# Moving the bit work of one weight pair, the scaling of low words, and the low half of an attention result in a fused attention and two-MLP kernel

## The chip, the cores and the metric

The kernel runs on one core of a Trainium2 chip. The metric is the device time of one execution in microseconds (us). Five engines work on their own instruction queues, each in order: TensorE (PE, with its weight loads shown as PEld), VectorE (DVE), ScalarE (ACT), GpSimd (POOL) and SyncE (SP), which issues the DMAs. An instruction starts when those before it on its queue are done and the semaphores that it waits for have come.

## The reference

All data are fp32; a local attention is followed by two feed-forward stages:

```
for each chunk c of 32 tokens (B=4, H=8, S=768, D=64):
    keys, values = 8 memory rows + 16 tokens to the left, the chunk, 8 to the right
    a = exp(scores - max(scores));  a = a / (sum(a) + 1e-9)
    out[c] = a @ values
x = out as 3072 tokens x 512
h = max(x @ w1, x @ w2, x @ w3)            # 512 -> 768
x = h @ w_mid                              # 768 -> 512
g = x @ w_in                               # 512 -> 2048
g = g where g >= 1, 0 where g <= -1, else (g + 1)^2 / 4
result = g @ w_out                         # 2048 -> 512
```

The weights (`w1`, `w2`, `w3`, `w_mid`, `w_in`, `w_out`) come in as float64 and are read by the kernel as pairs of 32-bit words, a low and a high one, from which it makes fp32.

## The kernel before

The 3072 tokens are six blocks of 512 (`TB`), and each block is four attention units of 128 tokens. The main matmuls are split in two halves: `mm3` (L538 to L541) multiplies high by high, low by high and high by low, so each product takes three matmuls of 128x512.

Blocks and units run like this. Attention units 0 to 7 and layer 1 of block 0 follow a written list (`PLAN`). Then a loop (L1088) goes over *slots*. A slot is one of the three layer-1 products of a sixth of the hidden width (`slot_l1`, with m = 0, 1, 2: twelve matmuls into one of two PSUM banks taken in turn by `next_mm`), or one layer-2 step (`slot_l2`, twelve matmuls). For m = 0 ACT copies the bank to `t` (L572), for m = 1 and 2 DVE takes the maximum with `t` (L574); the second slot of layer 1 after this one needs the bank again. After m = 2, in the next slot, ACT rounds `t` to `hh_a` (L556) and POOL subtracts to get `hl_a` (L558).

Behind its matmuls each slot of blocks 1 to 4 gets one step of an attention unit (`att_step`, `steps`; slots 2 and 3 get two), and the steps of one unit are six: (0) output `o` of the unit before on PE (L457), scores `s` on PE (L393), high half `cx` on ACT (L475), then on DVE the maximum and its subtraction `mx` (L407, L408) and the low half `dx` (L479), and on ACT the exponential `ex` (L412); (1) the normalising `n` on DVE (L416 to L419); (2) the rearrangement `pc` on ACT (L424, L427) and transposes for the next unit; (3) the transpose `ta` of the probabilities on DVE (L431), which `o` of the next step 0 reads; (4) and (5) little. The four `o` and `s` results share PSUM banks 4 and 5. Units 8 to 23 run here; the units whose step 0 lies in this loop are 9 to 23.

Beside it, `round_step` turns one pair of weight tiles in six slots into fp32, 16 pairs (12 to 27) in all. Action "a" takes absolute values of the high words on ACT (`abs_w`, L135), scales the low words on ACT (`tail_w`, L139) and works on the bits on DVE (`bits_w`, L143 to L146). Action "b" adds the low words on DVE (`sum_w`, L151) and combines (L159 to L162, or L176 to L179). `BY_PART` says which action falls to which of the six parts; "in" fetches the next weights, "out" stores the last, "p" splits a finished one on ACT (L169) and POOL (L170). The attention step comes ahead of `round_step` in a slot. Outside the pattern, "a" of pair 12 is put into slot 1 and its "b" into slot 3. In slots 0 and 1 ACT also empties four PSUM banks of block 0 (L605).

After block 4 the loop handles the last block without attention, and then the second feed-forward runs on PE to the end.

Of the kernel before, what the change touches and what calls it, by code (L numbers as in the profile page):

```python
# [65 lines left out]
def attention_then_two_mlps(ctx, tc, q, k, v, mem_k, mem_v, w1, w2, w3, w_mid, w_in, w_out, out):  # L66
# [17 lines left out]
    mx = ctx.enter_context(tc.tile_pool(name="mx", bufs=2))  # L84
# [25 lines left out]
    staged, split2, tiles = {}, {}, {}  # L110

    def fetch_w(n):
        q, i = divmod(n, 2)
        kind, j = conv[n]
        src = wsrc[kind]
        if q not in staged:
            staged[q] = stage.tile([P, 2, TB, 2], U32, tag="st", name=f"st{q}", bufs=2)
        st = staged[q][:, i]
        if kind in ("b", "d"):
            nc.sync.dma_start(out=st.rearrange("p f t -> p (f t)"), in_=src[j * P:(j + 1) * P, :])  # L120
        else:
            nc.sync.dma_start(
                out=st.rearrange("p (k f) t -> p k (f t)", k=KD),
                in_=src[:, 2 * j * P:2 * (j + 1) * P].rearrange("(k p) f -> p k f", p=P),
            )
# [8 lines left out]
    def abs_w(q, c):  # L134
        nc.scalar.activation(out=c.bitcast(F32), in_=staged[q][:, :, :, 1].bitcast(F32), func=AF.Abs)  # L135

    def tail_w(q):
        low = staged[q][:, :, :, 0]
        nc.scalar.activation(out=low, in_=low, func=AF.Copy, scale=2.0 ** -29)  # L139

    def bits_w(q, c):
        V, cf = nc.vector, c.bitcast(F32)
        V.tensor_scalar(out=cf, in0=cf, scalar1=LEAST, scalar2=MOST, op0=ALU.max, op1=ALU.min)  # L143
        V.tensor_scalar(out=c, in0=c, scalar1=3, scalar2=0x3FFFFFFF,
                        op0=ALU.logical_shift_left, op1=ALU.bitwise_and)
        V.scalar_tensor_tensor(out=c, in0=staged[q][:, :, :, 1], scalar=0xC0000000, in1=c,  # L146
                               op0=ALU.bitwise_and, op1=ALU.bitwise_or)

    def sum_w(q, c):
        st = staged.pop(q)  # L150
        nc.vector.tensor_tensor(out=c, in0=c, in1=st[:, :, :, 0], op=ALU.add)  # L151
        return st
# [12 lines left out]
    def streamed_d(c, d):  # L165

        for i, x in (0, d[:, 0:2]), (2, c[:, :, HK:]):
            hi = d[:, 3 + i:5 + i]
            nc.scalar.copy(out=hi.bitcast(F32R), in_=x)  # L169
            nc.gpsimd.tensor_tensor(out=x.bitcast(F32R), in0=x, in1=hi, op=ALU.subtract)  # L170
# [11 lines left out]
    def new_c(q):  # L182
        tiles[q] = stage.tile([P, 2, TB], U32, tag="c", name=f"c{q}", bufs=2)
        return tiles[q]
# [305 lines left out]
    def steps(u):  # L490
        old = u + 1 < TRIO0
        late = not old and u % 3 == 2
        if u == UB:
            yield [("s", u), ("mx", u), ("ex", u)]
        else:
            yield [("o", u - 1), ("s", u), ("cx", u - 1), ("mx", u), ("dx", u - 1), ("ex", u)]
        m = [("n", u)] + [("mv", u)] * (u % UPB == 0 or u == TURN0) + [("lv", u)]
        if old:
            v = [("tk", u + 2), ("ck", u + 2), ("ek", u + 2)] if u + 2 < TRIO0 else []
            v += [("lk", u + 4)] if u + 4 < TRIO0 else []  # L500
            yield m + v + [("kw", u + 1)]
            v = [("tq", u + 1), ("cq", u + 1)]
            v += [("lq", u + 3)] if u + 3 < TRIO0 else []
        else:
            yield m
            v = [("fk", u + 1)] * (not late)
        if u + 2 >= TRIO0:
            v += [("fq", u + 2)]
        if u == TRIO0 - 3 or u >= TRIO0 - 2 and u % 2 == 0:
            v += [("gq", u // 2 + 2)]  # L510
        if u >= TRIO0 - 2 and u % 3 == 1:
            v += [("gk", u // 3 + 1)]
        yield ([("pc", u)] if u >= TURN0 else []) + v
        yield [("ta", u)] if u >= TURN0 else [("a", u), ("ca", u)]
        new = u % UPB == 0
        yield [("fk", u + 1)] * late
        yield [("lm", u // UPB + 1)] if new and u < TURN0 else []
        if u == NU - 1:
            yield [("o", u), ("cx", u), ("dx", u)]
# [466 lines left out]
    def round_step(acts):  # L986
        if "out" in acts and kept:
            q, c, d = kept.pop(0)
            if q < Q2:
                f = q - Q1  # L990
                nc.sync.dma_start(out=sd[f], in_=d[:, 0:7])
                nc.sync.dma_start(out=sc[f].rearrange("p m f -> p (m f)"), in_=c.rearrange("p i f -> p (i f)"))
            else:
                nc.sync.dma_start(out=cd[q - Q2][:, 0:4].rearrange("p m f -> p (m f)"), in_=c.rearrange("p i f -> p (i f)"))
                nc.sync.dma_start(out=cd[q - Q2][:, 4:7], in_=d)
        if "p" in acts and kept and kept[0][0] < Q2:
            streamed_d(*kept[0][1:])
        q = rounded[0]
        if "a" in acts and q in staged:
            abs_w(q, new_c(q))  # L1000
            tail_w(q)
            bits_w(q, tiles[q])
        if "b" in acts and q in tiles:
            st = sum_w(q, tiles[q])
            c = tiles.pop(q).bitcast(F32)
            kept.append((q, c, (combine_d if q < Q2 else combine_w)(st, c)))
            rounded[0] += 1
        if "in" in acts:
            for _ in range(acts.count("in")):
                if fetched[0] < len(conv) and fetched[0] // 2 - rounded[0] < 2:  # L1010
                    fetch_w(fetched[0])
                    fetched[0] += 1

    BY_PART = "", "p", "", "out a", "in in", "b"

    with tc.manual_schedule(engines={ENG.PE, ENG.DVE, ENG.Activation, ENG.Pool, ENG.SP}):
        memk = at.tile([P, B // 2, 2, D], F32, tag="p", name="memk", bufs=2)
# [70 lines left out]
        for s, (f, *a) in enumerate(order):  # L1088
            j = a[0]
            if f is not slot_l2 and j == NB - 1 and last_block == 0:  # L1090
                while todo:
                    att_step()
                att.close()
                rp = ctx.enter_context(tc.tile_pool(name="rp", bufs=1, side="right"))
                last_block = s
                hb.append(rp.tile([P, TB], F32R, tag="hb0", name="hb0"))
                hb.extend(mx.tile([P, TB], F32R, tag="y", name=f"hb{i}", bufs=2) for i in (1, 2))
                fb.extend(rp.tile([P, TB], F32, tag=f"f{i}", name=f"f{i}") for i in range(6))
                hq["h12", 2] = [rp.tile([P, TB], F32, tag=f"h{i}", name=f"h12_{i}") for i in (4, 5)]
                for g in (0, 1):  # L1100
                    hq["h22", g] = rp.tile([P, 2, TB], F32, tag=f"a{g}", name=f"h22_{g}")
            made, out_now = unsplit[:], stores[:]
            del stores[:]
            f(*a)
            if last_block:
                made = unsplit[:]
            else:

                for _ in range(2 if s in (2, 3) else 1):
                    att_step()  # L1110
                    done += 1
                for _ in range(2):
                    if evictions:
                        evictions.pop(0)()

            for x in made:
                l1_split(*x)
                unsplit.remove(x)
            if last_block:
                t = s - last_block  # L1120
                round_step(["out"])
                if t == 1:
                    for g in (2, 3):
                        hq["h22", g] = w_tile(f"h22_{g}")
                for name in LAST_BLOCK.get(t, "").split():
                    if name == "c":
                        split_c()
                    elif name == "raw":
                        load_c(loaded[0])
                        loaded[0] += 1  # L1130
                    elif name == "r":
                        load_d(t - 4)
                    elif name == "d":
                        i = len(resident)
                        split_d(i)
                        if i + 2 < len(RESIDENT):
                            load_d(i + 2)
                    elif name == "E":
                        hq["h21", 0] = w_tile("h21_0")
                    else:  # L1140
                        prep(0, name)
            else:
                part = 5 if s == 3 else done % 6
                feed((5, 6, 4, 6, 5, 1)[part])
                round_step(BY_PART[part].split() + (["a"] if s == 1 else []))
                for store in out_now:
                    store()
        for x in unsplit:
# [81 lines left out]
```

## Time and profile before

| | |
|---|---|
| median of 3 runs | 962.69 us (959.14, 962.69 and 962.74) |
| profiled execution, its own time | 958.58 us |
| span of that execution, first to last instruction | 956.8 us |
| PE busy | 933.4 us, 98% of the span |
| DVE, ACT, POOL busy | 715.3, 569.9, 339.1 us |
| mean granted TensorE clock | 0.994 of full speed |

Times in the rows below are from the start of the span. PE's idle time is 23.4 us of the span. In a timeline row the first number is the start, the second the duration; in square brackets stands the idle time ahead of the instruction and what ended it. Slots 0 to 94 of the loop lie from about 125 to 423 us.

### The profile page before, as it was taken

How to read it: one execution, taken by the hardware profiler on the slowest of the kernel's cores; microseconds unless marked ns; L12 is line 12 of the kernel's file. 1: busy time of each engine (PE TensorE's matmuls, PEld its weight loads, DVE VectorE, ACT ScalarE, POOL GpSimd, SP SyncE). 2: the span in 40 equal slices, each digit the busy share in tenths (PEclk: the TensorE clock that was granted, in tenths of full speed). 3: DMA queues.
4: the chain of work that ended last, by engine and by line, in shares of the span. 5: the costliest groups of instructions: out<-in, count | busy, mean ns of one | idle time of the engine just before them, and what ended most of it. 6: DMA issues, size and time to landing. Idle time of an engine off the chain costs nothing.

```text
span 956.8 us, 18726 instructions
## 1 busy us (share of the span) xinstructions
PE 933.4 (98%) x7026; PEld 767.3 (80%) x7026; DVE 715.3 (75%) x1017; ACT 569.9 (60%) x1036; POOL 339.1 (35%) x330
## 2 busy tenths in 40 slices
PE   6799989999999999999999999999999999999998
PEld 5588877878888888888888888888888888888886
DVE  3999848788887878753337778997777998777854
ACT  5767544554454345333347777776777776776763
POOL 0000002322321111111646665555665555655542
PEclk8999999999999999999999999999999999999999
DMA  7896625776858677333424239514326744232823
GB/s 179 237 223 208 193 83 159 178 211 193 215 143 207 173 191 240 111 132 110 138 65 128 78 93 304 159 34 111 99 78 211 213 113 102 83 94 86 261 67 66
DMA packets 245548, 142.82 MB, mean 149 GB/s; under 512 B 174290, under 2 KB 223186, under 8 KB 245458
## 3 DMA queue, kind: packets, MB, share of 16 engines
q1 hardware_dynamic: 245458, 141.63, 52.7%
q8 instruction: 55, 0.90, 0.4%
q14 instruction: 35, 0.29, 0.1%
HBM read 109.87 MB, written 31.46 MB: 148 GB/s over the span
## 4 chain that ended last, share of the span: by engine, by line
PE 91%; DVE 4%; ACT 2%; SPq 1%; issue 1%; DMA 1%; POOL 0%; DVEq 0%; POOLq 0%; ACTq 0%
PE psums L539 29%; PE psums L541 28%; PE psums L540 28%; PE psums L393 2%; PE psums L457 2%; DMA kq<-in_k_dram 1%; PE psums L288 1%; DVE c L151 0%; PE psums L1051 0%; PE psums L464 0%; SPq L983 0%; SPq L375 0%; DVE p L408 0%; DVE few L407 0%; ACT c L135 0%
## 5 line engine op out<-in xcount | busy, mean ns | idle before, releaser
L558 POOL TENSOR_TENSOR hl_a<-t,hh_a 128x512 fp32r<-128x512 f32 x30 | 41.0, 1365 | 383.2 <-ACT hh_a L556 224.9
L539 PE MATMUL psums<-xh,hi 128*128 128x512 f32 x432 | 170.9, 396 | 1.4 <-ACT t L572 1.4
L540 PE MATMUL psums<-xl,hi 128*128 128x512 f32 x432 | 168.2, 389 | 0.4 <-DVE xl L479 0.4
L541 PE MATMUL psums<-xh,lo 128*128 128x512 f32 x432 | 168.6, 390 | 0.0
L850 POOL TENSOR_TENSOR hb<-h,hb 128x512 fp32r<-128x512 f32 x72 | 99.5, 1383 | 92.4 <-PE psums L541 59.7
L842 ACT CAST hb<-h 128x512 fp32r<-128x512 f32 x144 | 88.8, 622 | 48.1 <-PE psums L540 46.5
L574 DVE TENSOR_TENSOR t<-psums,t 128x512 f32<-128x512 f32 x72 | 49.4, 686 | 68.0 <-PE psums L541 67.9
L539 PEld LDWEIGHTS psums<-xh,hi 128*128 128x128 f32 x432 | 81.1, 188 | 19.1 <-ACT t L572 2.0
L669 POOL TENSOR_TENSOR hb<-ra,hb 128x256 fp32r<-128x256 f32 x96 | 75.4, 797 | 58.6 <-ACT hb L668 54.0
L541 PEld LDWEIGHTS psums<-xh,lo 128*128 128x128 f32 x432 | 81.1, 188 | 17.6 <-DVE lo L205 0.5
L540 PEld LDWEIGHTS psums<-xl,hi 128*128 128x128 f32 x432 | 81.2, 188 | 17.1 <-DVE xl L479 0.9
L734 ACT ACTIVATE psums<-h 128x512 f32<-128x512 f32 x96 | 57.9, 603 | 61.1 <-DVE h L820 24.3
L541 PE MATMUL psums<-t,hb 128*128 128x512 f32 x192 | 74.8, 390 | 0.0
L539 PE MATMUL psums<-t,hb 128*128 128x512 f32 x192 | 74.7, 389 | 0.0
L540 PE MATMUL psums<-t,hb 128*128 128x512 f32 x192 | 74.7, 389 | 0.0
L669 POOL TENSOR_TENSOR hb<-rb,hb 128x256 fp32r<-128x256 f32 x72 | 55.7, 780 | 39.4 <-ACT hb L668 39.4
L848 DVE TENSOR_TENSOR hb<-psums,hb 128x512 fp32r<-128x512 f32 x66 | 44.9, 680 | 24.8 <-PE psums L541 20.1
L735 ACT ACTIVATE psums<-psums 128x512 f32<-128x512 f32 x96 | 55.9, 582 | 3.1
L539 PE MATMUL psums<-hh_a,hi 128*128 128x512 f32 x144 | 57.5, 399 | 0.0
L875 DVE TENSOR_TENSOR h<-h,h 128x1024 f32<-128x1024 f32 (+1 forms) x42 | 56.5, 1368 | 0.0
L540 PE MATMUL psums<-hl_a,hi 128*128 128x512 f32 x144 | 56.2, 390 | 0.0
L541 PE MATMUL psums<-hh_a,lo 128*128 128x512 f32 x144 | 56.2, 390 | 0.0
(150 smaller groups left out, 2260.0 us busy)
## 6 DMA issues: line engine op xcount, KB each, us to landing
ra<-cd SPq DMA_DIRECT2D x24, 512.0 KB
st<-in_moe_w_out_dram SPq DMA_DIRECT2D x22, 512.0 KB
t<-sd SPq DMA_DIRECT2D x21, 512.0 KB
st<-in_moe_w_dram SPq DMA_DIRECT2D x18, 512.0 KB
st<-in_moe_w_in_dram SPq DMA_DIRECT2D x16, 512.0 KB
sd<-st SPq DMA_DIRECT2D x8, 896.0 KB
vw<-in_v_dram SPq DMA_DIRECT2D x59, 112.0 KB
h<-yd SPq DMA_DIRECT2D x12, 512.0 KB
```

What stands on the lines that cost most here:

```text
L539: nc.tensor.matmul(out, whi, xhi, start=first, stop=False)
L540: nc.tensor.matmul(out, whi, xlo, start=False, stop=False)
L541: nc.tensor.matmul(out, wlo, xhi, start=False, stop=last)
L558: e.tensor_tensor(out=lo, in0=h, in1=hi.bitcast(F32), op=ALU.subtract)
L574: nc.vector.tensor_tensor(out=cur["t", j, f], in0=s, in1=cur["t", j, f], op=ALU.max)
L669: nc.gpsimd.tensor_tensor(out=c[:, 1], in0=t, in1=c[:, 0].bitcast(F32), op=ALU.subtract)
L734: nc.scalar.activation(out=a, in_=x, func=AF.Relu, bias=0.5, scale=0.5)
L735: nc.scalar.activation(out=a, in_=a, func=AF.Square)
L842: nc.scalar.copy(out=hi, in_=x)
L848: nc.vector.tensor_tensor(out=lo, in0=y, in1=hi.bitcast(F32), op=ALU.subtract)
L850: nc.gpsimd.tensor_tensor(out=lo, in0=x, in1=hi.bitcast(F32), op=ALU.subtract)
L875: nc.vector.tensor_tensor(out=x, in0=y, in1=z, op=op)
```

## The change

Three things change. In `steps`, `dx` of the unit before stands ahead of `mx` on DVE's queue (it was behind it). In `round_step`, `tail_w` is taken out of action "a" and becomes action "t", which falls to the next part, together with "in". Action "a" of the first pair is issued in slot 2 and not in slot 1; its "t" falls into the same slot 2. `PLAN` is as it was.

```diff
-            yield [("o", u - 1), ("s", u), ("cx", u - 1), ("mx", u), ("dx", u - 1), ("ex", u)]
+            yield [("o", u - 1), ("s", u), ("cx", u - 1), ("dx", u - 1), ("mx", u), ("ex", u)]
...
         if "a" in acts and q in staged:
             abs_w(q, new_c(q))
+            bits_w(q, tiles[q])
+        if "t" in acts and q in tiles:
             tail_w(q)
-            bits_w(q, tiles[q])
...
-    BY_PART = "", "p", "", "out a", "in in", "b"
+    BY_PART = "", "p", "", "out a", "in in t", "b"
...
-                round_step(BY_PART[part].split() + (["a"] if s == 1 else []))
+                round_step(BY_PART[part].split() + (["a"] if s == 2 else []))
```

## Rows read from the trace of the kernel before

**Rows 1.** Waits of PE, 118 to 430 us: total us, times, longest.
```profile
PE psums L457 <- issue: 3.3, 1, 3.3
PE psums L539 <- ACT t L572: 1.4, 1, 1.4
PE psums L540 <- DVE xl L479: 0.4, 1, 0.4
```
**Rows 2.** Windows: stretch, length, busy us of each engine, PE clock, DMA share, GB/s.
```profile
140.00:145.00 5.00, 4.54 (x134) 4.13 (x135) 1.04 (x2) 0.59 (x1) 0.00 (x0) 0.66 0.26 60
...
220.00:430.00 210.00, 210.00 (x2259) 172.75 (x2252) 162.94 (x253) 90.18 (x151) 33.87 (x25) 1.00 0.64 178
```
**Rows 3.** Timeline of PE.
```profile
134.10 0.39 PE L541 MATMUL psums<-xh,lo 128*128 128x512 f32 x1
...
136.82 0.39 PE L541 MATMUL psums<-xh,lo 128*128 128x512 f32 x1
140.47 2.09 PE L457 MATMUL psums<-aT,vw 64*64 64x32 f32 x64 [3.26 <-issue]
...
143.55 0.50 PE L539 MATMUL psums<-xh,hi 128*128 128x512 f32 x1
...
150.01 0.48 PE L539 MATMUL psums<-hh_a,hi 128*128 128x512 f32 x1
...
158.07 0.39 PE L541 MATMUL psums<-xh,lo 128*128 128x512 f32 x1
159.82 0.50 PE L539 MATMUL psums<-xh,hi 128*128 128x512 f32 x1 [1.36 <-ACT t L572]
...
181.35 0.39 PE L541 MATMUL psums<-xh,lo 128*128 128x512 f32 x1
...
183.52 0.50 PE L539 MATMUL psums<-xh,hi 128*128 128x512 f32 x1
...
204.81 0.39 PE L539 MATMUL psums<-xh,hi 128*128 128x512 f32 x1
205.64 0.50 PE L540 MATMUL psums<-xl,hi 128*128 128x512 f32 x1 [0.44 <-DVE xl L479]
```
**Rows 4.** Single lines: engine, operation, count, ns min/median/max, first and last start.
```profile
L457 PEldq EVENT_SEMAPHORE  x6: 51/51/7314, 133.0 to 159.9; - x6
...
L407 DVE TENSOR_REDUCE few<-psums x15: 691/692/693, 144.3 to 406.2; 128x8 f32<-128x512 f32 x15
...
L419 DVE TENSOR_TENSOR p<-p,few x15: 691/694/1501, 152.2 to 410.2; 128x512 f32<-128x512 f32 x15
```
**Rows 5.** Timeline of DVE.
```profile
136.46 0.69 DVE L143 TENSOR_SCALAR c<-c 128x1024 f32<-128x1024 f32 x1 [4.36 <-ACT c L135]
...
139.06 0.68 DVE L574 TENSOR_TENSOR t<-psums,t 128x512 f32<-128x512 f32 x1
139.66 0.70 DVE L431 STREAM_TRANSPOSE aT<-pp 128x512 f32<-128x512 f32 x1
...
203.57 0.69 DVE L407 TENSOR_REDUCE few<-psums 128x8 f32<-128x512 f32 x1 [0.65 <-ACT xh L475]
...
204.90 0.68 DVE L479 TENSOR_TENSOR xl<-psums,xh 128x512 fp32r<-128x512 f32 x1
```
**Rows 6.** Timeline of ACT.
```profile
132.04 1.65 ACT L427 COPY pp<-p 32x256 f32<-32x256 f32 x4
...
135.31 1.12 ACT L135 ACTIVATE c<-st 128x1024 f32<-128x1024 f32 x1
...
157.16 1.12 ACT L135 ACTIVATE c<-st 128x1024 f32<-128x1024 f32 x1
158.17 1.13 ACT L139 ACTIVATE st<-st 128x1024 uint32<-128x1024 uint32 x1
159.19 0.58 ACT L572 COPY t<-psums 128x512 f32<-128x512 f32 x1
```
**Rows 7.** Timeline of POOL.
```profile
147.06 1.57 POOL L558 TENSOR_TENSOR hl_a<-t,hh_a 128x512 fp32r<-128x512 f32 x1 [145.61 <-DMA qs<-in_q_dram]
```

## The prediction, written before the changed kernel was run

> **What bounds the kernel now.** I read PE's waits first, because the table gives PE busy for 98% of the span. In the stretch where the changed steps run, PE waits only three times [rows 1]: 3.3 us ahead of an attention output (L457), 1.4 us ahead of a layer-1 product whose bank ACT had not emptied (L572), and 0.4 us for a low half (L479). Call them A, B and C. The windows say the rest: from 220 to 430 us PE is busy 210.00 of 210.00 us [rows 2], so nothing that DVE or ACT does there sets the end; an edit can win there nothing and lose only if it uses up slack. After that the PE queue runs nearly without a gap to the end, so what is won at A, B and C I carry to the end whole. Last I read the timelines around the three waits, to see which instruction ended each and what stood ahead of it.
>
> A is more than its 3.3 us. The same step, undisturbed, takes 183.52 - 181.35 = 2.17 us from the last matmul ahead of L457 to the first behind L393; at A it takes 143.55 - 136.82 = 6.73 us [rows 3]. So A costs 4.56 us: 3.26 us idle, and 1.30 us because the small matmuls behind the gap ran slower. The windows show the reason: the granted clock was 0.66 from 140 to 145 us [rows 2], a mixture of the 1.2 and 2.4 GHz levels after the idle time.
>
> What ended A? The trace writes "issue", which names nobody. But PE's queue for L457 sat in one semaphore wait of 7314 ns, begun at 133.0 [rows 4], so it came free at 133.0 + 7.3 = 140.3 or a little later, and DVE's transpose L431 ended at 139.66 + 0.70 = 140.36 [rows 5]. Its input was ready long before: the last of ACT's four L427 ended at 132.04 + 1.65 = 133.69 [rows 6]. L431 was late only because it stood on DVE behind L574, and L574 behind the bit work of pair 12, which began at 136.46 when ACT had finished the absolute values [rows 5, 6].
>
> **First pair a slot later.** Nothing is added or removed. In slot 1 the bit work (three instructions, from 136.46 until L574 starts at 139.06, so 2.60 us) stood ahead of slot 2's L574 and L431; now it stands behind them. L574 then waits for PE alone: slot 2's last matmul starts at 134.10 and takes 0.39, so L574 can start at about 134.6, and L431 follows 0.6 us later, as in the rows, and ends near 134.6 + 0.60 + 0.70 = 135.9 [rows 3, 5]. PE wants it at 140.47 - 3.26 = 137.21 [rows 3]. That leaves 1.3 us to spare, so A goes completely: **4.56 us**. The bit work itself is not delayed: ACT's absolute values still run at 135.31 to 136.43, because ACT has no idle time ahead of them, and DVE still starts at 136.46 [rows 5, 6]. It ends near 139.1; the cast L475, for which DVE waits next, can't start before `o` and `s` are through, at 137.21 + 2.17 - 0.23 = 139.2 (0.23 us is a matmul's turn, twelve from 134.10 to 136.82 [rows 3]). So it hides in DVE's wait for that cast. If that cover were gone, the maximum would come up to 2.6 us late, with no PE wait of its own but with B behind it. What is late next is the chain behind the cast, which now starts 4.5 us earlier as PE does. SP's queue sees no new or moved DMA: part 4 of slot 2 fetches nothing yet, as before, because two pairs are staged.
>
> **Low words a slot later.** L139 (16 times, 1.13 us) was queued between the absolute values and the next slot's L572. At B it is what kept L572 waiting: absolute values at 157.16, scaling at 158.17, L572 at 159.19, PE released at 159.82 where it could have gone on at 158.07 + 0.23 = 158.30 [rows 3, 6]. B costs 1.52 us. With the scaling behind L572, L572 starts 159.19 - 158.17 = 1.02 us earlier relative to that chain. The chain itself (cast, maximum, subtraction, sum, normalising, L427, absolute values) is serial work of DVE and ACT behind the cast, 13.6 us from 143.55 to 157.16 [rows 3, 6], so it moves with PE by 4.56 us, less, as I estimate it, 0.07 us for an ACT and a DVE that are now only just free. B is then 1.52 - 1.02 + 0.07 = 0.57 us: **0.95 us** saved. Bounds: 1.52 if the chain moves a little more than PE, 0 if it lags PE by a further 1 us, for which the 1.50 us that L419 takes at its slowest against 0.69 at its fastest is the nearest row [rows 4]. What the move may cost: the sum L151 waits for the scaling, and L572 ahead of it on ACT waits for its slot's matmuls. It stands a whole slot (2.7 us of matmuls, 136.82 - 134.10) later on DVE, against 0.58 + 1.13 us of ACT work [rows 3, 6], so about 1 us of room remains; I take nothing.
>
> **Low half ahead of the maximum.** Before, DVE ran L407 at 203.57, L408, then L479 at 204.90; PE stood from 204.81 + 0.23 = 205.04 to 205.64 for it [rows 3, 5]. L479 moves ahead by 204.90 - 203.57 = 1.33 us and ends near 204.25, 0.8 us before PE asks. C goes: 0.60 us, and about 0.1 us because the first matmul after a wait takes 0.50 us against 0.39: **0.70 us** (bounds 0.44 by the waits, 0.70). In return the maximum, the exponential and, where the rounding to `hh_a` stands behind the exponential on ACT, that too come 0.61 us later in 15 units [rows 4]. I price this at nothing. The tightest place is right behind A: POOL ends `hl_a` at 147.06 + 1.57 = 148.63, and PE first wants it at 150.01 [rows 3, 7]. Of these 1.4 us the swap takes 0.61 us, and 0.8 us is left. In the steady part PE's 210.00 of 210.00 us show no place where it now waits.
>
> **Sum.** 4.56 + 0.95 + 0.70 = 6.2 us. Against the profiled execution's own time, 958.58 - 6.2 = 952.4 us. The median of the three runs is 4.1 us above that execution, which gives 956.5. The four times known lie in two pairs, near 959 and near 962.7; I put the forecast a little on the side of the median: **955.0 us**. For this kernel 0.5% is 4.8 us, about what a measurement can tell from no change.
>
> **The clock part.** Of A's 4.56 us, 1.30 us is clock. The granted clock of 0.66 behind a gap of 3.26 us, and full clock behind the gap of 1.36 us (L539 at 159.82 takes 0.50 us like an undisturbed one at 183.52), are this trace's [rows 2, 3]. The Trainium skill ("TensorE: Matmul & The Clock Gate", Part 1: The HAM clock gate) says that what idleness and warming cost can differ from run to run of the same kernel, as the chip's look at activity is not tied to the program. By that rule some runs of the kernel before don't pay the 1.30 us, and the gain would be 4.9 us there; no run here shows it yet.
>
> **Rivals.** *Less than the sum* (0.18). B is not relieved, or the clock part was paid by this execution only. The first gives 4.56 + 0.70 = 5.3, the second 4.9, both together 4.0 us: 953.3 to 954.6 on the profiled execution's time, 957.4 to 958.7 on the median. For it: the chain behind the cast is 13.6 us of serial work, so a few tenths change B. I give each 0.09. Against: every link of it is in the timeline and none waits for a transfer.
>
> *Nothing happens at A* (0.06). Another semaphore than L431's is the last one, a load of `vw` for instance. Then B and C alone give at most 0.95 + 0.70 = 1.65 us: 956.9, or 961.0 on the median. For it: the trace says "issue". Against: 140.36 and 140.47 fit to 0.11 us.
>
> *Slower, by the swap* (0.05). If each of the 15 delayed maxima found no slack, PE would lose 0.61 us and 0.1 us of restart in each, 10.7 us in all; with the 6.2 us won that is +4.5 us: 963.0, or 967.1 on the median. It decides from 9 of 15 units (6.2 / 0.71 = 8.7). For it: the maximum heads each unit's chain through the exponential, L419, L427 and L431 to `o`. Against: 210.00 of 210.00 us, and the room of 0.8 us even at the tightest place. L419 took up to 1.50 us and 0.69 at best [rows 4]; one that is slowed where it was not costs DVE 0.8 us on top of the 0.61, more than such a room. For that the chance is 0.05 and not 0.03. The Trainium skill ("GPSIMD Engine Reference", 8. Key points) has GpSimd sharing its SBUF interfaces with VectorE, in contention when VectorE reads two SBUF inputs, as L419 does; by it an L419 that slips under POOL's work is slowed, and one that slips out of it gets quicker.
>
> **How the numbers follow.** The forecast's own case has 0.71: a gain of 5.6 to 6.8 us. With the runs' two levels that is 958.58 - 6.8 = 951.8 to 962.74 - 5.6 = 957.1. The lesser gains reach 958.7, no change at A 961.0. The range of 951.0 to 960.0 leaves out the slower case and the upper part of the third, and some scatter, together less than 0.2. For the sign: 6.2 us is only 1.4 us beyond the 4.8 us bound, and the runs shown differ by 3.6 us. Of the 0.71 I count 0.54 beyond the bound, of the 0.18 another 0.06; so faster 0.60. Slower by over 0.5% takes most units to lose their slack: 0.04. The rest, 0.36, is within 0.5%.
>
> **What would show it.** Right: PE's waits list no L457 wait in slot 3, the small matmuls of L457 there take about half their 2.09 us, and the clock shows no dip near 140; L431 stands on DVE ahead of L143 and ends near 136; B shrinks to 0.3 to 0.8 us with the scaling behind L572; L479 ends before PE wants `xl` and C is gone; 220 to 430 us stays full. Wrong: a wait for L457 of the old length with another releaser; B at 1.4 us or more; new waits for `hl_a`, or for L572 and L574, spread over the units.

## The result, and the profile after

The changed kernel takes 953.24 us in the median of five runs (952.52 to 955.89), the kernel before 961.9 us (959.14 to 962.74). The ratio is 0.9917 with a 95% interval of 0.9896 to 0.9938, so 6 to 10 us are gone. The forecast was 955.0 us in a range of 951.0 to 960.0, from a sum of 6.2 us.

PE's waits from 118 us to the end show what became of A, B and C [rows 1]. This is the view of PE's waits of the changed kernel; the second line belongs to the end of the program and was there before.

```profile
PE psums L539 <- ACT t L572: 0.3, 1, 0.3
PE psums L931 <- DVE f L929: 0.2, 1, 0.2
```

A and C are gone, and of B 0.3 us idle is left. The windows of the changed kernel at the same places [rows 2]:

```profile
140.00:145.00 5.00, 5.00 (x143) 4.05 (x142) 4.19 (x6) 2.24 (x4) 0.00 (x0) 1.00 0.57 146
...
220.00:430.00 210.00, 210.00 (x2174) 172.93 (x2173) 163.97 (x253) 90.69 (x151) 33.67 (x25) 1.00 0.65 176
```

The clock stays at 1.00 where it was 0.66, and PE is as full from 220 to 430 us as it was. PE's timeline of the changed kernel around the three places [rows 3], and the queue's own wait for L457 [rows 4]:

```profile
132.03 0.47 PE L539 MATMUL psums<-xh,hi 128*128 128x512 f32 x1
...
140.53 0.39 PE L541 MATMUL psums<-xh,lo 128*128 128x512 f32 x1
140.85 1.14 PE L457 MATMUL psums<-aT,vw 64*64 64x32 f32 x64
...
142.71 0.50 PE L539 MATMUL psums<-xh,hi 128*128 128x512 f32 x1
...
145.58 0.60 PE L288 MATMUL psums<-ident,kq 128*128 128x128 f32 x4
...
157.17 0.39 PE L541 MATMUL psums<-xh,lo 128*128 128x512 f32 x1
157.91 0.50 PE L539 MATMUL psums<-xh,hi 128*128 128x512 f32 x1 [0.35 <-ACT t L572]
...
202.89 0.39 PE L539 MATMUL psums<-xh,hi 128*128 128x512 f32 x1
203.11 0.40 PE L540 MATMUL psums<-xl,hi 128*128 128x512 f32 x1
```

```profile
L457 PEldq EVENT_SEMAPHORE  x5: 51/51/51, 136.7 to 158.0; - x5
```

From the last matmul ahead of L457 to the first behind L393 are now 142.71 - 140.53 = 2.18 us; they were 6.73. No semaphore wait of L457 is longer than 0.05 us; one was 7.3. At B the pause is 157.91 - 157.17 - 0.23 = 0.51 us against 1.52. At C the first matmul that needs `xl` follows after 0.22 us; it was 0.83. DVE and ACT show the reasons. First DVE, then ACT, of the changed kernel [rows 5, 6]:

```profile
138.24 0.69 DVE L574 TENSOR_TENSOR t<-psums,t 128x512 f32<-128x512 f32 x1 [2.42 <-PE psums L541]
138.85 0.70 DVE L431 STREAM_TRANSPOSE aT<-pp 128x512 f32<-128x512 f32 x1
140.19 0.69 DVE L143 TENSOR_SCALAR c<-c 128x1024 f32<-128x1024 f32 x1 [0.64 <-ACT c L135]
...
144.76 0.69 DVE L408 TENSOR_TENSOR p<-psums,few 128x512 f32<-128x512 f32 x1
...
202.23 0.69 DVE L479 TENSOR_TENSOR xl<-psums,xh 128x512 fp32r<-128x512 f32 x1 [0.65 <-ACT xh L475]
```

```profile
156.25 1.13 ACT L135 ACTIVATE c<-st 128x1024 f32<-128x1024 f32 x1
157.29 0.56 ACT L572 COPY t<-psums 128x512 f32<-128x512 f32 x1
157.76 1.16 ACT L139 ACTIVATE st<-st 128x1024 uint32<-128x1024 uint32 x1
```

L431 stands ahead of the bit work and ends at 139.55, 1.3 us before PE asks. L572 stands ahead of the scaling. L479 ends at 202.23 + 0.69 = 202.92, and PE takes `xl` at 203.11, so 0.2 us are to spare, where 0.8 were forecast.

All times after lie later than one would think, because this execution's loop began late: slot 1's first matmul started at 132.03, and at 128.31 in the profiled execution of before. So I compare *loop length*, from that matmul to the first matmul of the last attention output: 421.88 - 128.31 = 293.57 us before, 419.15 - 132.03 = 287.12 us after, 6.45 us less. Behind the loop both take the same, 956.8 - 421.88 = 534.92 and 954.1 - 419.15 = 534.95 us. What comes before the loop was not changed. These are the windows of the first 60 us, of the kernel before and then of the changed one:

```profile
0.00:30.00 30.00, 21.40 (x467) 16.86 (x468) 13.74 (x34) 17.30 (x32) 0.85 (x8) 0.89 0.87 209
30.00:60.00 30.00, 24.45 (x434) 19.64 (x433) 29.16 (x42) 21.11 (x30) 0.00 (x0) 1.00 0.82 204
```

```profile
0.00:30.00 30.00, 19.79 (x388) 15.15 (x393) 11.80 (x30) 14.64 (x30) 0.85 (x8) 0.80 0.80 198
30.00:60.00 30.00, 25.58 (x515) 20.92 (x502) 28.65 (x42) 20.88 (x29) 0.00 (x0) 0.86 0.80 199
```

PE is idle nearly as long in both (60 - 21.40 - 24.45 = 14.15 us and 60 - 19.79 - 25.58 = 14.63 us), but the clock was lower in the second: 0.83 over the 60 us against 0.94, and PE got through less. Over the 13 profiles of the table below the start goes with this clock, from 0.91 and 0.94 (starts of 128.2 to 129.3) down to 0.80 (131.4 and 132.2), and not with PE's idle time in these 60 us (12.0 to 15.1 us). What sets that clock in an execution was not tested.

### The profile page after: what moved, and what is told of

It reads as the page before. It is cut to its first block, busy times and chain, and to the rows that moved or that the text cites. A ratio compares the mean times of both kernels' runs of the same rounds, so it can differ in the third digit from the quotient of the medians.

```text
span 954.1 us, 18733 instructions
## 1 busy us (share of the span) xinstructions
PE 934.9 (98%) x7026; PEld 769.4 (81%) x7026; DVE 717.1 (75%) x1017; ACT 568.9 (60%) x1036; POOL 338.3 (35%) x330
## 4 chain that ended last, share of the span: by engine, by line
PE 93%; DMA 2%; SPq 2%; DVE 1%; ACT 1%; issue 0%
PE psums L539 30%; PE psums L541 29%; PE psums L540 29%; PE psums L457 2%; PE psums L393 2%; DMA kq<-in_q_dram 1%; SPq L122 1%; PE psums L319 0%; DMA st<-in_moe_w_dram 0%; PE psums L288 0%; PE psums L464 0%; DMA kq<-in_k_dram 0%; DMA vxl<-in_v_dram 0%; SPq L280 0%; DVE c L151 0%
```

## The experiments

All of them start from the changed kernel, save two that are the kernel before once more. "Start" is slot 1's first matmul, "loop" the loop length; both are of the profiled execution. The ratio is to the kernel before, timed on the same chip; before's median was 960.05 us in 18 runs beside the first four experiments of the table, and 960.56 us in 19 runs beside the others that have a ratio. A single run has no ratio, and its time also holds the scatter of the start.

| | start | loop | median us | ratio, 95% interval |
|---|---|---|---|---|
| before | 128.31 | 293.57 | 961.9 | |
| before, second profile | 129.34 | 293.90 | 959.96 (1 run) | |
| before, third profile | 128.25 | 294.65 | 959.64 (1 run) | |
| changed | 132.03 | 287.12 | 953.24 | 0.9917 (0.9896 to 0.9938) |
| changed, second profile | 129.14 | 287.26 | 953.10 (1 run) | |
| first pair back in slot 1 | 130.09 | 292.42 | 959.97 | 0.9995 (0.9982 to 1.0008) |
| scaling back | 131.39 | 288.23 | 954.67 | 0.9949 (0.9932 to 0.9966) |
| low half back | 129.80 | 287.86 | 954.64 | 0.9944 (0.9925 to 0.9963) |
| absolute values early | 128.21 | 287.19 | 952.98 | 0.9930 (0.9909 to 0.9950) |
| one third of the bit work late | 130.69 | 290.46 | 957.12 | 0.9961 (0.9949 to 0.9974) |
| maximum three times | 131.18 | 294.50 | 961.26 | 1.0012 (0.9999 to 1.0025) |
| maximum twice | 132.16 | 288.79 | 957.99 (1 run) | |
| sum of the first pair later | 130.74 | 286.45 | 954.25 | 0.9933 (0.9917 to 0.9948) |

### The first pair back in slot 1

```diff
-                round_step(BY_PART[part].split() + (["a"] if s == 2 else []))
+                round_step(BY_PART[part].split() + (["a"] if s == 1 else []))
```

> The first pair's bit work and absolute values go back to slot 1; the other two parts of the change stay. Measure: loop length, from slot 1's first layer-1 matmul to the first matmul of the last attention output (293.57 us before the change, 287.12 after). Theory (the transpose L431 behind the bit work on DVE's queue is the whole of A): the wait for L457 in slot 3 is back with about 3.3 us idle and the slower small matmuls behind it, loop length up by 4.5 to 4.6, to about 291.7. Rival (the cost of the clock belonged to that one execution): up by 3.3 only, to 290.4. Rival (A was a load of vw that happened to be early in the changed kernel's run): no change, 287.1. Device time against the kernel before: about 0.998 by the theory.

A is back with the same idle time to the hundredth. PE's timeline of this kernel, and its windows (length, PE busy, clock, DMA share, GB/s):

```profile
142.24 2.10 PE L457 MATMUL psums<-aT,vw 64*64 64x32 f32 x64 [3.26 <-issue]
```

```profile
141.00:142.00 1.00, 0.00 (x0) 0.67 0.00 0
142.00:143.00 1.00, 0.76 (x25) 0.50 0.00 0
...
147.00:148.00 1.00, 1.00 (x4) 0.50 1.17 230
148.00:149.00 1.00, 1.00 (x5) 0.92 0.27 36
```

But the loop grew by 5.30 us and not by 4.55. The reader sees why in the clock: it stayed at half until about 148, six microseconds behind the start of L457, and the layer-1 slot behind it ran slow. PE was then so late that B's wait vanished, though its chain was the same. So the rival of a load of `vw` falls, the idle time is as the theory has it, and the price of the clock was neither fixed nor smaller, but larger. The device time's ratio of 0.9995 says that without this part the other two are worth too little to be timed.

### The scaling back

```diff
         if "a" in acts and q in staged:
             abs_w(q, new_c(q))
+            tail_w(q)
             bits_w(q, tiles[q])
-        if "t" in acts and q in tiles:
-            tail_w(q)
```

> The scaling of the low words goes back behind the absolute values in the same slot (action a); the other two parts stay. Theory (the scaling ahead of L572 on ACT's queue is what keeps the bank at B): B's wait grows from 0.5 us (0.51 lost in the changed kernel) by 1.0, loop length 288.1. Rival (with A gone, ACT's chain has room and the scaling costs nothing): 287.1, with L572 as early as now.

The loop is 1.11 us longer, and PE waits 1.4 us at B. The theory holds; A's room did not help ACT's chain.

```profile
158.31 0.50 PE L539 MATMUL psums<-xh,hi 128*128 128x512 f32 x1 [1.39 <-ACT t L572]
```

### The low half back behind the maximum

```diff
-            yield [("o", u - 1), ("s", u), ("cx", u - 1), ("dx", u - 1), ("mx", u), ("ex", u)]
+            yield [("o", u - 1), ("s", u), ("cx", u - 1), ("mx", u), ("dx", u - 1), ("ex", u)]
```

> The low half goes back behind the maximum; the other two parts stay. Theory (C is the position of L479 alone): the wait for xl at the head of block 2 is back, loop length up by 0.6 to 0.7, to 287.8, and nothing else changes although 15 maxima come 0.6 us earlier. Rival (the swap costs something in other units, hidden in the balance): up by clearly less than 0.6, or down. Rival (C is covered once A and B are gone, as PE and DVE stand differently to each other): no change, 287.1.

The loop is 0.74 us longer and C is back, so the whole 0.7 us of C reaches the end and the swap costs nothing elsewhere that shows.

```profile
201.44 0.50 PE L540 MATMUL psums<-xl,hi 128*128 128x512 f32 x1 [0.40 <-DVE xl L479]
```

### Absolute values early, bit work late

```diff
         if "a" in acts and q in staged:
             abs_w(q, new_c(q))
-            bits_w(q, tiles[q])
+            if s != 1:
+                bits_w(q, tiles[q])
+        if s == 2:
+            bits_w(q, tiles[q])
...
+                round_step(BY_PART[part].split() + (["a"] if s == 1 else []))
```

> The first pair's absolute values (ACT) are issued in slot 1 again, its three bit instructions (DVE) stay in slot 2. Theory (only the place of the bit work on DVE's queue matters): A stays away, loop length 287.1. Rival (ACT's place counts too, as absolute values in slot 1 stand ahead of slot 2's and 3's work on ACT): a part of the 4.55 us is back, loop length 288 or more.

The loop is 287.19 us, as in the changed kernel, and L457 waits for nothing. A was a matter of DVE's queue alone: ACT's place in it counts for nothing.

### One third of the bit work late

L143 and L144 stay in slot 1, L146 (here `bits_3`, which `bits_w` leaves out in slot 1) goes behind the transpose in slot 2.

```diff
             abs_w(q, new_c(q))
-            bits_w(q, tiles[q])
+            bits_w(q, tiles[q], s == 1)
+        if s == 2:
+            bits_3(q, tiles[q])
...
+                round_step(BY_PART[part].split() + (["a"] if s == 1 else []))
```

> As in the kernel before, the first pair's absolute values and its first two bit instructions (L143, L144) are issued in slot 1; only the third (L146) waits until slot 2, behind the transpose. The transpose then comes 139.06 - 137.92 = 1.14 us earlier than before the change, so A's idle time should be 3.26 - 1.14 = 2.1 us. Theory (the clock falls only behind a long gap; it stayed full behind 1.36 us and fell behind 3.26): the clock stays full, loop length 287.12 + 2.1 + 0.1 = 289.3, less up to 0.5 that B then no longer costs. Rival (it falls behind this gap too): 1 to 2.5 us more, 290.3 to 291.8.

The idle time is 1.99 us, as expected, but the theory on the clock falls: the loop is 290.46 us long, in the rival's range. In the windows the clock is still full while PE is idle and for at least 1.4 us after it works again, and then falls (PE's timeline first; its line numbers are four higher here, so L461 is L457):

```profile
141.58 1.39 PE L461 MATMUL psums<-aT,vw 64*64 64x32 f32 x64 [1.99 <-issue]
```

```profile
140.00:141.00 1.00, 0.00 (x0) 1.00 0.00 0
...
142.00:143.00 1.00, 1.00 (x70) 1.00 0.07 16
143.00:144.00 1.00, 1.00 (x65) 0.78 0.03 7
144.00:145.00 1.00, 1.00 (x3) 0.50 0.47 107
...
146.00:147.00 1.00, 1.00 (x3) 0.51 1.13 242
147.00:148.00 1.00, 1.00 (x6) 1.00 0.40 56
```

### The maximum three times, and twice

The second kernel has 2 in place of 3. The result is the same; DVE's work ahead of the exponential grows by 1.44 and 0.72 us in each of 15 units.

```diff
-        nc.vector.tensor_reduce(out=m, in_=sg, axis=AX.X, op=ALU.max)
+        for _ in range(3 if u > TURN0 else 1):
+            nc.vector.tensor_reduce(out=m, in_=sg, axis=AX.X, op=ALU.max)
```

> The changed kernel with the maximum (L407) computed three times over in each of the 15 units, the same result each time: DVE's work ahead of the subtraction and the exponential grows by 1.44 us a unit. Theory (the delay that the swap brings is hidden, with a room of about 1 us at the tightest place, the split of slot 2 behind A, and none at B): two places pay, the split by about 0.3 us and B by about 1.2 us, loop length about 288.5. Rival (no room in the units: each delay of the maximum reaches PE): up by 15 x 1.44 = 21.6 us, to 308.7; with room in half of them some 298.

I expected 288.5 us and measured 294.50: the theory was far too hopeful, though the rival with 308.7 is farther off. PE's waits of this kernel from 118 to 430 us (lines one higher):

```profile
PE psums L540 <- ACT t L573: 2.3, 5, 0.9
PE psums L288 <- DVE p L409: 1.2, 1, 1.2
PE psums L540 <- ACT xh L476: 0.9, 1, 0.9
PE psums L541 <- DVE xl L480: 0.2, 1, 0.2
```

These eight waits sum to 4.6 us idle. Matmul by matmul against the changed kernel, PE falls behind by 0.2 to 0.4 us more than the listed idle time at seven of them (the eighth is B's, which the changed kernel has too) and by 0.1 to 0.4 us at four places where no wait is listed; that makes up the 7.4 us. Neither `hl_a` nor its split is among them. The second line is one I hadn't thought of: unit 11's transposes (L288) write the bank from which unit 9's scores are still read. In the changed kernel the subtraction L408 ends at 144.76 + 0.69 = 145.45 and the transposes start at 145.58, with 0.13 us of room. So half the dose came next.

> The changed kernel with the maximum computed twice over in each of the 15 units (three times cost 7.4 us of loop length where 1.4 was expected): DVE's work ahead of the exponential grows by 0.72 us a unit. Theory now (each place has a room of its own; the tightest is the transposes of unit 11 behind the subtraction of unit 9, whose bank they share, with 0.1 us left in the changed kernel, and the others that failed at 1.44 us have between 0.5 and 1.4): the transposes wait about 0.6 us, one or two places more lose some tenths, loop length 287.8 to 288.8. Rival (no room anywhere, PE pays in proportion): half of 7.4, loop length 290.8.

The loop is 288.79 us, at the upper edge of what was expected and 2 us below the rival's. PE's waits, then PE's timeline at the head of block 2, where C was:

```profile
PE psums L288 <- DVE p L409: 0.5, 1, 0.5
PE psums L540 <- ACT t L573: 0.4, 1, 0.4
PE psums L541 <- DVE xl L480: 0.2, 1, 0.2
PE psums L540 <- ACT xh L476: 0.2, 1, 0.2
```

```profile
204.07 0.51 PE L540 MATMUL psums<-xh,hi 128*128 128x512 f32 x1 [0.18 <-ACT xh L476]
204.79 0.51 PE L541 MATMUL psums<-xl,hi 128*128 128x512 f32 x1 [0.22 <-DVE xl L480]
```

0.72 us a unit cost PE 1.7 us in all, 1.44 us a unit 7.4 us. Matmul by matmul against the changed kernel, the 1.7 us are 0.7 at unit 11's transposes and 1.0 at the head of block 2; behind that nothing is lost, and from 220 to 430 us PE is still busy 210.00 of 210.00 us. With 1.44 us a unit it is busy 208.21 us there. So two places have a room of less than 0.72 us, and several more have less than 1.44. The swap's 0.61 us fits in everywhere, at the transposes by 0.13 us and at C by 0.2.

### The first pair's sum later

```diff
-                part = 5 if s == 3 else done % 6
+                part = done % 6
...
-        if "p" in acts and kept and kept[0][0] < Q2:
+        if "p" in acts and kept and kept[0][0] < Q2 and s != 4:
...
+                round_step(BY_PART[part].split() + {2: ["a"], 4: ["b"], 5: ["p"]}.get(s, []))
```

> The changed kernel with the first pair's sum and combination (DVE, about 4 us) moved from slot 3 to slot 4, behind the normalising of unit 9, and the splitting of its result from slot 4 to slot 5. Theory (what is left of B comes from that work standing in front of unit 9's normalising, and so in front of L427, the absolute values and L572): B is gone, loop length 287.12 - 0.5 = 286.6, about 0.05% in device time, less than can be timed. Rival (the sum now delays the L574 of slot 5 and with it the bank of slot 8, or the split): a new wait of up to 1 us, loop length 287.1 to 288.

The loop is 286.45 us, 0.67 less than in the changed kernel, and PE waits nowhere from 118 to 430 us. On ACT, L572 now waits for PE and not PE for it:

```profile
152.31 1.12 ACT L135 ACTIVATE c<-st 128x1024 f32<-128x1024 f32 x1
153.64 0.59 ACT L572 COPY t<-psums 128x512 f32<-128x512 f32 x1 [0.21 <-PE psums L541]
```

In device time this is not to be told from the changed kernel: 0.9933 (0.9917 to 0.9948) beside 0.9917 (0.9896 to 0.9938).

### Both kernels again

> The kernel before, unchanged, once more with a profile. Theory (A's idle time is fixed by the queues, but what the clock adds differs from execution to execution): 3.26 us idle at L457 again within 0.1, and a stretch at half clock behind it of another length than the 3.3 us of the first profile; loop length between 293 and 295.5. Rival (the clock part is as fixed as the idle time): loop length 293.57 within 0.1. The start of the loop, slot 1's first matmul, may lie anywhere from 128 to 132 us by both.

> The kernel before a third time with a profile. Theory (the half-clock stretch behind A differs from execution to execution; what it adds beyond the first profile's is mostly taken back at B, because B's chain starts at the cast and not at PE): 3.26 us idle at A, half clock for 3 to 7 us, B's wait the shorter the longer that stretch is, loop length 293.5 to 294.2. Rival (the clock's cost goes to the end in full): loop length up by as much as the half-clock stretch is longer, 294.6 or more for a stretch of 6 us.

> The changed kernel, unchanged, once more with a profile. Theory: loop length 287.12 within 0.1, no wait but B's; what differs between executions is the start of the loop, anywhere from 128 to 132 us, by the waits for the loads of the first 60 us; the span is the loop's start plus its length plus 534.95. Rival (the start of 132.03 belongs to the changed kernel): the start is near 132 again.

A's idle time was 3.26 us in all three profiles of before. The clock was not the same. Windows of the second profile of before:

```profile
141.00:142.00 1.00, 0.51 (x15) 0.50 0.00 0
...
146.00:147.00 1.00, 1.00 (x4) 0.50 1.25 205
147.00:148.00 1.00, 1.00 (x4) 0.61 0.64 88
```

From slot 1's first matmul to unit 11's transposes the first profile took 146.42 - 128.31 = 18.11 us, the second 19.59 and the third 19.48, against 145.58 - 132.03 = 13.55 after. A cost 4.56, 6.04 and 5.93 us there. But the first matmul behind B came 31.51, 31.91 and 31.81 us after the start: of the 1.4 us that the clock took beyond the first profile only 0.3 to 0.4 remained, since B, whose chain hangs on the cast and not on PE, shrank from 1.52 to 0.48 and 0.51 us. The first of these three expectations held. The third profile's loop was 294.65 and not 294.2 or less; that is no matter of the clock, but of a wait that the others don't have, for a weight load that came late. ACT's timeline there, then PE's:

```profile
343.56 1.13 ACT L135 ACTIVATE c<-st 128x1024 f32<-128x1024 f32 x1 [3.16 <-DMA st<-in_moe_w_in_dram]
344.59 1.15 ACT L139 ACTIVATE st<-st 128x1024 uint32<-128x1024 uint32 x1
345.61 0.59 ACT L572 COPY t<-psums 128x512 f32<-128x512 f32 x1
```

```profile
346.26 0.50 PE L539 MATMUL psums<-xh,hi 128*128 128x512 f32 x1 [0.52 <-ACT t L572]
```

Here too the scaling stood ahead of L572. With the scaling behind it, as in the changed kernel, this wait would have had 1.02 us more room; in neither profile of the changed kernel does a load come late enough to test it, so that is argued and not shown. The second profile of the changed kernel has a loop of 287.26 us (0.04 us more than expected), B's wait of 0.34 us and nothing else, and its start was 129.14: the late start belonged to one execution. The expectation put the scatter of the start down to the waits for the first loads; the windows of the first 60 us put it down to the clock, as said above.

## Why the prediction was right, and where it was not

**A.** 4.56 us forecast, 4.55 measured between the two first profiles (6.73 - 2.18). That they agree to the hundredth is in part luck, as the forecast was read from the same execution of before; in the other two A cost 6.04 and 5.93 us. Its cause was the transpose behind the bit work on DVE, as said: with only the bit work moved it goes, with only the third instruction moved its idle time falls by 1.27 us, and with all of it moved back it returns. The rival by which nothing happens at A is gone.

**The clock part.** This step was wrong in sign. I let 1.30 us stand as the price or as something that some runs don't pay, and gave 0.09 to a smaller gain from it. Every profile with the gap paid it, and two of before's three, and the experiment that restored A, paid about 1.4 us more. The Trainium skill ("TensorE: Matmul & The Clock Gate", Part 1: The HAM clock gate) has the cost of warming up differ from run to run of one kernel; the traces agree that it differs, with half clock for some 3 us in one execution and for 6 to 7 us in three. My reading of it, that some runs of before escape, no run showed.

**B.** 0.95 us forecast, 1.01 measured between the two first profiles (1.52 to 0.51), and 1.11 us with the scaling put back. The chain behind the cast moved with PE. But how A and B share the gain belongs to the execution: in the other two of before B cost 0.48 and 0.51 us, no more than after, and A more. Their sum is steadier: to the first matmul behind B it is 31.51, 31.91 and 31.81 us before, and 157.91 - 132.03 = 25.88 after, so 5.6 to 6.0 us against 5.51 forecast.

**C.** 0.70 us forecast, 0.74 with the low half put back. The room behind it was mis-sized, 0.2 us and not 0.8: the forecast set L479 at L407's old place, but with the swap DVE comes there 0.6 us later. With the low half put back L407 starts 1.28 us ahead of the first matmul of block 2 (199.37 and 200.65), in the changed kernel L479 only 0.66 us (202.23 and 202.89).

**The swap at no cost.** Right as a sum, wrong in its reason. The tightest place was not `hl_a` with 0.8 us, but the shared bank of the transposes with 0.13 us, which I had not followed; C's 0.2 us come next. The argument from PE's full 210 us held for that stretch, where even 0.72 us more a unit costs nothing; but it does not give the size of the room, which falls short at 1.44, and it says nothing of the places ahead of 206 us, where 0.72 us more costs 1.7 us. The rival "slower, by the swap" did not come; even 1.44 us more a unit cost 7.4 us and not 15 x 1.44 = 21.6.

**The sum and the point.** The three terms gave 6.2 us; the loop lost 6.45 us between the first profiles, and 6.85 us between the means of all profiles (294.04 of three before, 287.19 of two after). The late load of the third profile is 0.7 us of its loop; without it the means differ by 6.6 us. The medians of larger timings agree: 960.05 of 18 runs against 953.24 of the first comparison's five is 6.8 us. The first comparison's 8 us is a little more than that, and its interval reaches down to 6. The two levels of the runs, on which I set the point of 955.0, are not there in the 18 runs, which lie scattered from 958.3 to 962.7. The scatter comes from the start, which lies between 128.21 and 132.16 us over 13 profiles, in kernels whose program up to there is the same: start, loop and 536.7 us make up the profiled time in twelve of the 13, and 537.0 in one. No run of before above 960 us has a profile. The point was 1.8 us too high, because I leaned towards the upper level.

## What to carry to other kernels

A queue in order turns the place of a cheap instruction into a wait on the busiest engine: look behind each of PE's few waits for the instruction on the other queue that stood ahead of the one waited for, and move that. Two waits in a row need not add up: when the first grew by 1.4 us the second shrank by 1.0, and a relieved first one shows up in the second unless its chain moves along. And a full PE shows that nothing waits, not by how much: the room must be read at every consumer, the owners of shared PSUM banks included, or measured by doubling an operation.

## What the runs showed of the hardware

The clock's answer to an idle PE differed in its moment and in its length. Behind the gaps of 3.26 us the granted clock was at half before PE worked again (0.67 in the idle microsecond from 141 us with the first pair back in slot 1). Behind one gap of 1.99 us it fell only after PE had worked for more than a microsecond again. Half clock then lasted some 3 us behind the shorter gap and in one execution with the longer one, and 6 to 7 us in three. Behind the gaps of 1.36 and 1.39 us at B the windows show no dip. So the gaps of 2 and 3.3 us cost more than their idle time, here 1.3 to 2.8 us more up to unit 11's transposes, of which B took back up to 1.0, and that part is not to be read from one profile.

The same holds for the start of a program: up to the loop 13 executions of the same instructions differed by 4 us, with a granted clock from 0.80 to 0.94 over the first 60 us.
